# Hedgehog attention and a maxout feed-forward: two heads' last query tokens in one padded tile, part of the first q over a plain queue, and a new order table

## Chip, cores and metric

The kernel runs on one core of one Trainium2 chip. The metric is the device time of one execution in microseconds (us), and lower is better. TensorE is called PE here, VectorE DVE, ScalarE ACT, GpSimd POOL; SyncE (SP) issues transfers only. In a row of the profile, `out<-in` names the tile that is written and the tile that is read, and `L748` is line 748 of the kernel.

## What is computed

Linear attention with a learned feature map, and after it a feed-forward whose hidden layer is the maximum of three products. q, k and v are [8 batches, 8 heads, 576 tokens, 64] in fp32, the hidden width is 768, and the output is [4608, 512].

```python
def phi(x):
    proj = np.einsum('bhsd,df->bhsf', x, w_phi)
    proj = proj - np.max(np.abs(proj), axis=-1, keepdims=True)
    return np.concatenate([np.exp(proj), np.exp(-proj)], axis=-1)
q_p, k_p = (phi(q), phi(k))
kv = np.einsum('bhsf,bhsd->bhfd', k_p, v)
z = np.sum(k_p, axis=2)
num = np.einsum('bhsf,bhfd->bhsd', q_p, kv)
den = np.einsum('bhsf,bhf->bhs', q_p, z)[..., None] + 1e-06
attn = num / den                      # then the heads of a token side by side: x [4608, 512]
h = np.maximum(np.maximum(x @ w1, x @ w2), x @ w3)
return h @ w_out
```

## The kernel before

**Units and chunks.** The attention is done in 16 units: a unit is one batch and four of its eight heads, so units 2b and 2b+1 make batch b. Of a head's 576 tokens 512 are its main tokens, that is four tiles of 128, and the last 64 are its tail. The feed-forward runs in nine chunks of 512 tokens: chunks 0 to 7 take the main tokens of one batch each, chunk 8 the tails of all eight batches.

**Loads.** q and k of a unit are cast to bf16 by the transfer that loads them (`qk_bf`, L383 and L393, issued by POOL). Only unit 0's k comes in as fp32 over SP (`k_raw`, L408) and is cast by DVE and ACT (L415). The tails of q come as fp32 over SP (`tail_raw`, L426, two issues for each pair of units), and POOL casts them into `qk_bf` (L430). v comes as fp32 (`v_raw`, L435).

**Attention of a unit.** Head dimension onto partitions: for units 0 to 3 PE transposes `qk_bf` (`tps`, L459) and DVE or ACT copies the result (`qkT`, L470 and L472); later units use a transposing transfer that SP issues (L478). Then `psk`, `psq`, `pst` = tokens times w_phi (L496), with only 64 of PE's rows in use; the largest magnitude of each token by DVE (`mk`, `mq`, L500); exp of the k features by ACT (`Ek`, L504); v scaled by the tokens' factors `em` on POOL (`vab`, L548); `kvps` = k features times scaled v (L567, 64 rows), copied to `kv_sb` (L574). For q the projection is made the other way round, so that its features lie on partitions (`psm`, L593 with 64 rows, and L600 for the tails), and ACT takes exp of it (`Eq`, L584). The numerators and the denominator are `psn` = Eq times kv_sb (L632), 65 columns for each tile of 128 tokens. They are worked in groups of five tiles, one group for a head: its four main tiles, and the tile that holds its tail and that of its neighbour, of which half goes unused. That makes four groups and 40 matmuls for a unit. DVE joins the two signs (`y`, L641 and L644), inverts the denominator (`rden`, L689), and POOL divides (`x_sb`, L690).

**From x to the output.** x is turned again (`xT`): for units 0 and 1 by PE (`pxT`, L707, copied at L718), and for the others by a transposing transfer of ten blocks (L722, SP). A chunk of the feed-forward takes `ups` = xT times a weight (L748, four matmuls for each of 12 tiles; the first weight enters as differences `w2-w1` and `w3-w1`, made on POOL at L844, and a product of w1 and w_out made once, L855 to L869). DVE or ACT evacuates (L758, L762, L764), then `ops` = the straight product (L781) and the product with w_out (L786), its copy `osb` (L796) and its store (L800, on SP or ACT). The tails of a batch are copied into chunk 8's operand by POOL (L896, L897).

**What sets the order.** Every piece of work is a node, and the table `PLAN` lists all nodes in one sequence, with the engine, the buffers and a time for each; `plan` (L205) reads it. Each engine works through its own nodes in that sequence, and SP's sequence is its queue. So nothing overtakes anything on one engine: an instruction that waits holds up whatever stands behind it there. `fill` (L222) puts matmuls on dummy data (`idler`, L911) between PE's first nodes, where the table's times leave room.

Of the kernel before, what the change touches and what calls it, by code (L numbers as in the profile page):

```python
# [19 lines left out]
P = 128  # L20
# [12 lines left out]
XW = SM + P  # L33
# [4 lines left out]
BY_HALF = 0  # L38
BY_BATCH = 99
# [10 lines left out]
TRAW = 2  # L50
WD_PE = 0
# [37 lines left out]
9G0@1.2 10S0@0.8 3A@1.1 1D@0.8 2G@1.9 16S0@1.3 0G@2.1 103G1@2.7 104G@7.2 4A@1.8 12D@4.0 8G@7.5 6D@4.2 11A@4.0  # L89
19T0@4.5 5A@4.3 7A@4.6 20D0@5.2 25T1@5.8 187S1@2.9 13S@4.5 26D@6.4 29T23@6.3 102G@8.2 30A0@6.7 51T45@6.9 73T67@7.1 110T0@8.0  # L90
105S1@5.1 34A0@7.2 106T1@8.1 18S2@5.7 53D0@7.3 33A@7.7 32D0@7.9 35D@8.5 107D1@9.1 119T53@9.9 75A0@8.2 31A@8.7 260G2@8.9 77A@9.1
74A0@9.6 186G3@9.6 259G@10.4 111D@9.7 76A@10.1 112T21@10.1 188G@11.1 124A1@10.6 123A1@11.1 126T06@10.3 52D@9.9 128A@11.5 17G@11.3 122D1@10.5
115D@11.1 127A@11.8 1166G@11.5 15D@11.7 27T4@12.1 14D@12.0 117A@12.1 120A@12.5 121A@13.0 1167G@12.3 1169G@13.0 130D1@12.2 28D@12.5 43T76@12.8
21T4@13.0 261G@13.8 129D@12.7 46D@13.1 47D@13.5 54A0@13.6 113A@13.8 78T0@13.3 22D@13.8 36T56@14.3 118D@14.1 125D@14.7 56G0@14.0 44A@14.3
114A@14.5 79A@15.0 23T4@14.6 39D@15.3 40A@15.3 24D@15.9 42D@16.3 48T23@16.4 55G@15.1 137A1@15.8 139G1@16.2 80A@16.0 45A@16.2 50D@16.9
116A@16.5 185G@17.3 58A@17.0 108T4@16.7 37A@17.2 334S0@11.6 140G@18.0 263T0@17.2 57A@17.7 59G@18.2 60G@19.3 267T7@17.7 68T13@17.9 61G@20.4
38A@17.8 49D@17.5 81A0@18.3 109D@18.1 264D2@18.7 268D@19.3 41A@18.5 72A@18.9 71A@19.4 138G@20.5 141A@19.9 131T25@18.8 142G@21.6 144A@20.1
62T46@19.1 64A0@20.2 69A@20.3 63A@20.8 70A@21.0 134T07@19.7 132D@19.5 190T3@20.1 65T26@20.6 1168G@22.7 133D@20.1 156T54@21.2 135D@20.7 82T01@21.6
67A@21.4 66A@21.6 161T6@21.9 136D@21.3 158A1@21.7 191D3@21.8 85T27@22.1 159A1@22.2 143G@23.4 83D0@22.4 160A@22.7 86D@22.9 333G0@24.5 157A@23.2
# [156 lines left out]
def kernel(  # L256
# [686 lines left out]
```

## Time and profile before

| | |
|---|---|
| median of three runs | 281.54 us (281.24, 284.22, 281.54) |
| the profiled execution | 282.56 us |
| its span | 280.8 us, so 1.76 us lie around it |
| PE busy | 268.3 us |
| DVE, ACT, POOL busy | 217.3, 199.1, 161.5 us |
| granted clock of PE | 1.0 throughout |

The page gives the busy time of each engine and the span in 40 slices. Groups of instructions have their count, busy time and mean duration. The chain of waits goes back from the last instruction, at each step to what released it. A row of the timeline has start, duration, engine, line and operation. Rows by windows give each engine's busy time in a stretch. An engine that is busy in this sense may still hold a dummy matmul, or a matmul whose end is modelled.

### The profile page before, as it was taken

Reading aid. Unit: us, or ns where it says so; the run is one execution under the profiler, and the core shown is the slowest. Engines: PE = TensorE matmul, PEld = TensorE weight load, DVE = VectorE, ACT = ScalarE, POOL = GpSimd, SP = SyncE. Lnnn points to the kernel's source line nnn. Section 1 sums busy time; section 2 is a strip of 40 time slices with the busy share of each in tenths; the row PEclk is TensorE's granted clock in tenths of the full one; section 3 lists DMA queues with packets and bytes.
Section 4 is the critical chain, followed back from the end, with each engine's and each line's share of the span. In section 5 each row is a group of like instructions: output and inputs, shape, how many; then the busy total and the mean of one; then the engine's idle time right before and its main releaser. Section 6 shows DMA issues by size and latency. Waiting matters only on the chain. (4 is left out here: it accounts for less than half of the span.)

```text
span 280.8 us, 8401 instructions
## 1 busy us (share of the span) xinstructions
PE 268.3 (96%) x3409; PEld 150.8 (54%) x3447; DVE 217.3 (77%) x442; ACT 199.1 (71%) x489; POOL 161.5 (58%) x161
## 2 busy tenths in 40 slices
PE   8789899999999999999999999999999999999993
PEld 5457654576655555555555456655546544444441
DVE  2799989999999969889997899898876871157320
ACT  4799999999999787698978879989589200310001
POOL 4879999998949703897336848393495341000000
PEclk9999999999999999999999999999999999999999
DMA  7999999997999999999999997717130224110253
GB/s 136 300 202 208 207 173 310 260 164 132 171 186 249 236 196 281 169 171 144 189 263 204 188 276 125 151 55 170 39 86 3 77 47 121 40 75 0 82 144 112
DMA packets 76214, 44.52 MB, mean 159 GB/s; under 512 B 52688, under 2 KB 67344, under 8 KB 76176
## 3 DMA queue, kind: packets, MB, share of 16 engines
q1 hardware_dynamic: 59536, 29.21, 49.8%
q0 software_dynamic: 14912, 11.77, 28.7%
q10 hardware_dynamic: 1728, 3.02, 3.0%
q8 instruction: 27, 0.44, 0.7%
q14 instruction: 11, 0.09, 0.1%
HBM read 34.64 MB, written 9.44 MB: 157 GB/s over the span
## 5 line engine op out<-in xcount | busy, mean ns | idle before, releaser
L748 PE MATMUL ups<-xT,w_bf 128*128 128x512 bf16 x414 | 101.3, 379 | 1.0
L584 ACT ACTIVATE Eq<-psm 128x512 bf16<-128x512 f32 (+1 forms) x160 | 81.7, 587 | 5.4 <-PE psm L593 3.1
L548 POOL TENSOR_TENSOR vab<-v_raw,em 128x1152 bf16<-128x1152 f32 (+1 forms) x36 | 68.2, 1907 | 22.9 <-ACT em L542 15.0
L504 ACT ACTIVATE Ek<-psk 128x512 bf16<-128x512 f32 x128 | 72.1, 633 | 8.2 <-PE psk L496 6.3
L748 PEld LDWEIGHTS <-w_bf 128*128 128x128 bf16 x432 | 39.2, 98 | 43.9 <-issue 2.3
L690 POOL TENSOR_TENSOR x_sb<-y,rden 128x640 bf16<-128x640 f32 x32 | 39.9, 1256 | 39.5 <-DVE rden L689 39.0
L786 PE MATMUL ops<-wout_bf,hT 128*128 128x512 bf16 (+2 forms) x214 | 50.5, 373 | 0.3
L758 DVE TENSOR_TENSOR hT<-hT,ups 128x512 bf16<-128x512 bf16 x54 | 35.5, 677 | 13.3 <-PE ups L748 11.1
L500 DVE TENSOR_REDUCE mq<-psq 128x4 f32<-128x512 f32 x64 | 41.2, 682 | 3.5 <-PE psq L496 3.2
L500 DVE TENSOR_REDUCE mk<-psk 128x4 f32<-128x512 f32 x64 | 41.9, 679 | 2.1 <-PE psk L496 1.7
L762 ACT ACTIVATE hT<-ups 128x512 bf16<-128x512 f32 x36 | 21.9, 620 | 24.5 <-PE ups L748 24.4
L641 DVE TENSOR_TENSOR y<-psn,sq 128x325 f32<-128x325 f32 x64 | 30.4, 491 | 6.7 <-PE psn L632 4.3
L796 ACT COPY osb<-ops 128x512 f32<-128x512 f32 x20 | 12.2, 608 | 32.3 <-PE ops L786 31.8
L786 PEld LDWEIGHTS <-hT 128*128 128x128 bf16 x222 | 20.6, 98 | 22.5 <-issue 0.2
L632 PEld LDWEIGHTS <-Eq 128*128 128x128 bf16 x640 | 26.3, 98 | 10.3 <-issue 0.4
L644 DVE TENSOR_TENSOR y<-y,psn 128x325 f32<-128x325 f32 x64 | 29.7, 487 | 1.6
L632 PE MATMUL psn<-kv_sb,Eq 128*128 128x65 bf16 x640 | 28.8, 194 | 0.2
L496 PEld LDWEIGHTS <-qkT 64*128 64x128 bf16 x576 | 18.0, 94 | 13.4 <-issue 8.3
L781 PE MATMUL ops<-xT 128*128 128x512 bf16 x87 | 23.7, 380 | 0.5
L567 PE MATMUL kvps<-vab,Ek 64*128 64x65 bf16 x1152 | 22.1, 191 | 0.8 <-POOL vab L548 0.6
L567 PEld LDWEIGHTS <-Ek 64*128 64x128 bf16 x1152 | 20.3, 94 | 3.4 <-issue 1.3
L796 DVE COPY osb<-ops 128x512 f32<-128x512 f32 (+2 forms) x17 | 11.1, 657 | 12.5 <-PE ops L786 12.5
(65 smaller groups left out, 263.9 us busy)
## 6 DMA issues: line engine op xcount, KB each, us to landing
v_raw<-in_v_dram SPq DMA_DIRECT2D x15, 576.0 KB, 6.0
out_dram<-osb SPq DMA_DIRECT2D x23, 256.0 KB, 3.3
qk_bf<-in_k_dram POOLq DMA_DIRECT2D x15, 288.0 KB, 6.9
qk_bf<-in_q_dram POOLq DMA_DIRECT2D x15, 256.0 KB, 8.7
w_bf<-in_moe_w_dram POOLq DMA_DIRECT2D x3, 768.0 KB, 13.2
out_dram<-osb ACTq DMA_DIRECT2D x9, 256.0 KB, 3.4
tail_raw<-in_q_dram SPq DMA_DIRECT2D x16, 64.0 KB, 4.8
wout_bf<-in_moe_w_out_dram POOLq DMA_DIRECT2D x1, 768.0 KB, 19.2
```

What stands on the lines that cost most here:

```text
L500: return nd(kind, {"DVE": 0.598 if n == 4 else 0.331}, lambda: nc.vector.tensor_reduce(dst(m()), ps()[:, 0:n, :], AXX, ALU.max, apply_abso ...
L504: return nd("ek", {"ACT": 0.478 if n == 4 else 0.264}, lambda: nc.scalar.activation(dst(Ek[g]()), ps()[:, 0:n, :], EXP, scale=1.0 - 2.0 * ...
L548: made.append(chosen(n_, lambda n_, g=g, t0=t0, t1=t1: (nc.vector if n_.eng == "DVE" else nc.gpsimd).tensor_tensor(vab()[:, g, t0:t1, 0:D] ...
L567: nc.tensor.matmul(kvps[ab]()[:, pr, g, :], lhsT=Ek[g]()[r, t, :], rhs=vab()[r, g, t, :], start=(pr == prs[0] and g + j == 0), stop=(pr == ...
L584: return nd("eq", {"ACT": 0.478 if n == 4 else 0.264}, lambda: nc.scalar.activation(Eq[g]()[:, t0:t0 + n, :], ps()[:, 0:n, :], EXP, scale= ...
L632: nc.tensor.matmul(psn[g]()[:, i, :], lhsT=Eq[g]()[:, t, :], rhs=kv()[:, pr, ab, g, :], start=True, stop=True)
L641: n_ = nd("xu", {"DVE": 0.064 + 0.0676 * n_t}, lambda: nc.vector.tensor_tensor(yv(y()), ps(0), sq_of(sq()).unsqueeze(len(shape) - 1).to_br ...
L644: return nd("xw", {"DVE": 0.064 + 0.0674 * n_t}, lambda: nc.vector.tensor_tensor(yv(y()), yv(y()), ps(1), ALU.add), [n_], [psn[1], y], loc ...
L690: divs[pr] = nd("x", {"POOL": 1.2}, lambda pr=pr, y=y, rden=rden: nc.gpsimd.tensor_tensor(x_sb()[:, pr].rearrange("p t a d -> p a t d"), y ...
L748: nc.tensor.matmul(ups()[:, o * n:(o + 1) * n], lhsT=w_bf[i + (not plain)][:, ct, jj * P:(jj + 1) * P], rhs=tokens_of(ct)[:, cols] if halv ...
L758: nc.vector.tensor_tensor(dst, dst, src, ALU.max)
L786: nc.tensor.matmul(ops_()[:, 0:hi - lo], lhsT=hT()[:, j, tt * P:(tt + 1) * P], rhs=wout_bf[:, j, lo:hi], start=plain and j == 0, stop=(j = ...
```

## The change

- **Tails.** The tail tiles of two heads are combined before the numerators. `eq_ends` holds exp of the tails' q features with 64 zeroed columns between two heads' tails, so that an operand of 128 columns has one head's tail and zeros beside it. Two matmuls add up into one tile, which then has the tails of two heads. A unit so has 18 tiles instead of 20, still with 40 matmuls.
- **Groups.** Numerators go in three groups of six tiles (390 columns) instead of four of five (325), and two of them are main tiles only. DVE's join, the inverse and POOL's division have three pieces for a unit; the division had two. `sq` takes one activation instead of two. xT has nine blocks for a unit instead of ten, and PE turns units 0 and 1 in three groups of three blocks. The copy at the tails' end into chunk 8's operand takes one instruction instead of two.
- **Loads and stores.** q of the first two heads of unit 0 comes as fp32 over SP (`q_raw`) and DVE casts it in two pieces. Tails are loaded for each unit, two issues of 32 KB, where it was two of 64 KB for two units; there are four buffers for them instead of two. For units 0 to 3 the tails' cast may go to DVE or ACT, and the scaling of v to DVE. All of v and all full stores are issued by SP; before, one v and nine of these stores were on ACT.
- **Order.** `PLAN` is new throughout. Options that had been switched off are gone from the code.

The diff, cut to its core; of the table it shows one line each.

```diff
-XW = SM + P
+XB = PT * P
...
+PLAIN_Q = 1
...
-TRAW = 2
+TRAW = 4
...
-9G0@1.2 10S0@0.8 3A@1.1 1D@0.8 2G@1.9 16S0@1.3 0G@2.1 103G1@2.7 104G@7.2 4A@1.8 12D@4.0 8G@7.5 6D@4.2 11A@4.0
+13S0@0.8 1D@0.8 4A@1.1 0G@1.2 16S@1.3 3G@1.7 5A@1.8 19S0@1.9 12G0@2.2 2G@2.9 107G1@3.1 266S1@3.5 14D@4.0 7A@4.1
...
-    xT = const.tile([P, B, CT, XW], BF16, name="xT")
+    xT = const.tile([P, B, 2, XB], BF16, name="xT")
+    eq_ends = const.tile([P, ES, 2, 2, 3, ST], BF16, name="eq_ends")
...
+    n_zero = node("zero", 0, {"DVE": 0.25, "POOL": 0.45}, None, [], [], port=True)
+    chosen(n_zero, lambda n_: (nc.vector if n_.eng == "DVE" else nc.gpsimd).memset(
+        eq_ends.rearrange("p e g r z c -> p (e g r) z c")[:, :, 1, :], 0.0))
...
+        for p0, p1 in ((0, 1), (1, 2)) if u == 0 else ((0, 2),):
+            if u > 0 or p0 >= PLAIN_Q:
+                main_q.append([nd("Lq", {"POOL": 0.72}, lambda p0=p0, p1=p1: load_q(p0, p1), [], [qk_b],
+                                  xfer=[(16 * (p1 - p0), 44.0, 0.72)])])
+                continue
+            n_ = nd("Lq", {"SP": 0.42, "ACT": 0.58}, None, [], [qraw], xfer=[(16, 44.0, 0.42)])
+            chosen(n_, lambda n_, p0=p0: queue_of[n_.eng].dma_start(
+                qraw()[:, 8 * p0:8 * p0 + 8, :].rearrange("p (h j) d -> p h (j d)", j=SM // P),
+                q[b, h0 + 2 * p0:h0 + 2 * p0 + 2, 0:SM, :].rearrange("h (p j) d -> p h (j d)", p=P)))
+            parts = []
+            for t0 in (8 * p0, 8 * p0 + 4):
+                c_ = nd("Cq", {"DVE": 0.206, "ACT": 0.3}, None, [n_], [qraw, qk_b], port=True)
+                parts.append(chosen(c_, lambda c_, t0=t0: copy_on[c_.eng](qs()[:, t0:t0 + 4, :], qraw()[:, t0:t0 + 4, :])))
+            main_q.append(parts)
...
-        if u % 2 == 0:
-            t_raw = tails["raw"] = buf("tail_raw", TRAW, [P, 2 * HU // 2, D], FP32)
-
-            def load_t(n_):
-                ends = q[b, :, SM:S, :].rearrange("(pr ab) i d -> ab i pr d", ab=2)
-                for ab in range(2):
-                    queue_of[n_.eng].dma_start(t_raw()[ab * D:(ab + 1) * D, :, :], ends[ab])
-            tails["load"] = chosen(nd("Lt", {"SP": 1.24}, None, [], [t_raw], xfer=[(16, 18.0, 0.62)] * 2), load_t)
-        t_raw = tails["raw"]
-        n_ = nd("C", {"POOL": 0.233}, None, [tails["load"]], [t_raw, qk_b], port=True)
+        t_raw = buf("tail_raw", TRAW, [P, 2, D], FP32)
+
...
+        def load_t(n_):
+
+            ends = q[b, h0:h0 + HU, SM:S, :].rearrange("(a r) i d -> a i r d", r=2)
+            for a in range(2):
+                queue_of[n_.eng].dma_start(t_raw()[a * ST:(a + 1) * ST], ends[a])
+        n_t = chosen(nd("Lt", {"SP": 1.24}, None, [], [t_raw], xfer=[(8, 18.0, 0.62)] * 2), load_t)
+        n_ = nd("C", {"POOL": 0.24, "DVE": 0.13, "ACT": 0.17} if by_pe else {"POOL": 0.24}, None, [n_t], [t_raw, qk_b], port=True)
         tail = chosen(n_, lambda n_: copy_on[n_.eng](
             ks().rearrange("p (r j) d -> p r j d", j=PT + 1)[:, :, PT, :],
-            t_raw()[:, 2 * (u % 2):2 * (u % 2) + 2, :]))
+            t_raw()))
         vraw = buf("v_raw", RAW, [P, UT, D], FP32, of="raw")
-        main_v = chosen(nd("Lv", {"SP": 0.42, "ACT": 0.6}, None, [], [vraw], xfer=[(16, 93.0, 0.42)]),
+        main_v = chosen(nd("Lv", {"SP": 0.42}, None, [], [vraw], xfer=[(16, 93.0, 0.42)]),
                         lambda n_: queue_of[n_.eng].dma_start(
...
+                if u < BY_PE:
+                    costs["DVE"] = 0.064 + 0.0667 * (t1 - t0)
                 n_ = nd("va", costs, None, [n_em, main_v], [vraw, em, vab], port=True)
                 made.append(chosen(n_, lambda n_, g=g, t0=t0, t1=t1: (nc.vector if n_.eng == "DVE" else nc.gpsimd).tensor_tensor(
...
-        eqs["t"] = [q_exp(a, psm, 2, g, NQ) for g in range(2)]
-        x_sb = buf("x_sb", XSB, [P, 2, 5, 2, D], BF16)
...
+        eqs["t"] = [nd("eq", {"ACT": 0.264}, lambda g=g: nc.scalar.activation(
+            Et()[:, g, :, 0:3:2, :], psm()[:, 0:2, :].rearrange("p r (z c) -> p r z c", z=2), EXP, scale=1.0 - 2.0 * g),
+                       [a, n_tab], [psm, Et], locks=[psm]) for g in range(2)]
+
+
+        sq = buf("sq", MS, [P, UT], FP32)
+        n_sq = nd("S", {"ACT": 0.1}, lambda: nc.scalar.activation(sq(), mq(), EXP, scale=-2.0), reds_q, [mq, sq])
+        x_sb = buf("x_sb", XSB, [P, UT, D], BF16)
+        divs = []
+        for th in range(3):
+            mine = range(6 * th, 6 * th + 6)
+            ends = th == 2
+            prs = range(2) if ends else sorted({t // 8 for t in mine})
+            psn = [bank("psn", [P, 6, W]) for _ in range(2)]
+
+            def nmm(mine=mine, psn=psn):
+                for i, t in enumerate(mine):
+                    for g in range(2):
+                        o = psn[g]()[:, i, :]
+                        if t < NQ:
+                            pr, c, ab = t // 8, t // 2 % 4, t % 2
+                            nc.tensor.matmul(o, lhsT=Eq[g]()[:, 8 * (c % 2) + 4 * pr + 2 * ab + c // 2, :], rhs=kv()[:, pr, ab, g, :],
                                              start=True, stop=True)
-                        i += 1
...
+                            continue
+                        for pr in range(2):
+                            pad = Et()[:, g, t - NQ, pr:pr + 2, :].rearrange("p z c -> p (z c)")
+                            nc.tensor.matmul(o, lhsT=pad, rhs=kv()[:, pr, t - NQ, g, :], start=(pr == 0), stop=(pr == 1))
+            need = [n for pr in prs for n in n_kvs[pr]] + [n for pr in ((1,) if ends else prs) for n in eqs[pr]]
+            a = nd("N", {"PE": 0.0313 * (16 if ends else 12)}, nmm, need + (eqs["t"] + [n_zero] if ends else []),
+                   Eq + [kv] + [Et] * ends + psn)
+            y = buf("y", YS, [P, 6, W], FP32)
+            rden = buf("rden", YS, [P, 6, 1], FP32)
+            n_ = nd("xu", {"DVE": 0.064 + 0.0676 * 6}, lambda th=th, y=y, psn=psn: nc.vector.tensor_tensor(
+                y(), psn[0](), sq()[:, 6 * th:6 * th + 6].unsqueeze(2).to_broadcast([P, 6, W]), ALU.mult), [a, n_sq], [psn[0], sq, y],
                     locks=[psn[0]])
...
+            n_ = nd("xw", {"DVE": 0.064 + 0.0674 * 6}, lambda y=y, psn=psn: nc.vector.tensor_tensor(y(), y(), psn[1](), ALU.add),
+                    [n_], [psn[1], y], locks=[psn[1]])
+            n_ = nd("xr", {"DVE": 0.108}, lambda y=y, rden=rden: nc.vector.reciprocal(rden(), y()[:, :, D:W]), [n_], [y, rden])
+            n_ = nd("x", {"POOL": 0.767, "DVE": 0.464} if by_pe else {"POOL": 0.767}, None, [n_], [y, rden, x_sb], port=True)
+            divs.append(chosen(n_, lambda n_, th=th, y=y, rden=rden: (nc.vector if n_.eng == "DVE" else nc.gpsimd).tensor_tensor(
+                x_sb()[:, 6 * th:6 * th + 6, :], y()[:, :, 0:D], rden().to_broadcast([P, 6, D]), ALU.mult)))
 
...
+            for th in range(3):
+                pxT = bank("pxT", [P, 3, P], BF16)
+                def tx(th=th, pxT=pxT):
+                    for o in range(3):
+                        t = 6 * th + 2 * o
+                        nc.tensor.transpose(pxT()[:, o, :], x_sb()[:, t:t + 2, :].rearrange("p a d -> p (a d)"), ident)
...
+                nc.sync.dma_start_transpose(out=xT[:, b, u % 2, :].rearrange("p (t c) -> p t c", c=P),
+                                            in_=x_sb().rearrange("p t d -> p (t d)"))
+            done.append(nd("X", {"SP": 1.21}, xdma, divs, [x_sb], xfer=[(72, 18.0, 1.21)]))
...
-                    s_ = ff("store", {"SP": 0.41, "ACT": 0.6} if n_out == 1 else {"SP": 1.2}, None, [e], [osb],
+                    s_ = ff("store", {"SP": 0.41} if n_out == 1 else {"SP": 1.2}, None, [e], [osb],
...
     def last(b):
-        nc.gpsimd.tensor_copy(xT[D:P, b, :, SM:SM + ST], xT[D:P, b, :, SM + ST:XW])
-        nc.gpsimd.tensor_copy(x_last[b // 4][:, :, b % 4 * ST:(b % 4 + 1) * ST], xT[:, b, :, SM:SM + ST])
+        nc.gpsimd.tensor_copy(x_last[b // 4][:, :, b % 4 * ST:(b % 4 + 1) * ST].rearrange("p (u c) n -> p u c n", u=2),
+                              xT[:, b, :, 2 * SM:XB].rearrange("p u (c n) -> p u c n", n=ST))
     for b in range(B):
-        lasts.append(node("C", 2 * b + 1, {"POOL": 0.8}, lambda b=b: last(b),
+        lasts.append(node("C", 2 * b + 1, {"POOL": 0.42}, lambda b=b: last(b),
```

At the start of DVE's sequence the table changes what stands between unit 0 and unit 1. Names: `qk_bf<-k_raw` is unit 0's k, the copies `qkT<-tps` are transposed blocks, the reductions `mk`, `mq` the largest magnitudes. Before, from the first cast on:

```order
L415 CAST qk_bf<-k_raw 128x320
L337 CAST wph<-wphi_f 64x128
L472 COPY qkT<-tps 128x512 x2
L500 TENSOR_REDUCE mq<-psq 128x4
L500 TENSOR_REDUCE mk<-psk 128x4 x2
L470 COPY qkT<-tps 128x2x512
L470 COPY qkT<-tps 128x2x128
L500 TENSOR_REDUCE mq<-psq 128x4
```

After, the same place:

```order
L407 CAST qk_bf<-k_raw 128x256
L341 CAST wph<-wphi_f 64x128
L461 COPY qkT<-tps 128x512
L341 CAST wph_low<-wphi_f 64x128
L491 TENSOR_REDUCE mk<-psk 128x4 x2
L459 COPY qkT<-tps 128x2x128
L461 COPY qkT<-tps 128x512
L491 TENSOR_REDUCE mk<-pst 128x2
L461 COPY qkT<-tps 128x512
L491 TENSOR_REDUCE mq<-pst 128x2
L491 TENSOR_REDUCE mk<-psk 128x4
L459 COPY qkT<-tps 128x2x512
```

The first copy of `128x2x512`, which is unit 1's k, had five instructions ahead of it after the first two casts; now it has ten, unit 0's tail and the second half of its k among them.

The second place is SP's sequence around the transposing transfers of x of units 2 and 3 (`xT<-x_sb`). Before:

```order
L478 DMA_TRANSPOSE qkT<-qk_bf 128x10x128
L435 DMA v_raw<-in_v_dram 128x2x576 x2
L478 DMA_TRANSPOSE qkT<-qk_bf 128x8x128
L722 DMA_TRANSPOSE xT<-x_sb 128x10x128
L478 DMA_TRANSPOSE qkT<-qk_bf 128x10x128
L478 DMA_TRANSPOSE qkT<-qk_bf 128x8x128
L722 DMA_TRANSPOSE xT<-x_sb 128x10x128
L478 DMA_TRANSPOSE qkT<-qk_bf 128x10x128
```

After:

```order
L467 DMA_TRANSPOSE qkT<-qk_bf 128x10x128
L426 DMA v_raw<-in_v_dram 128x2x576
L418 DMA tail_raw<-in_q_dram 64x2x64 x2
L426 DMA v_raw<-in_v_dram 128x2x576
L467 DMA_TRANSPOSE qkT<-qk_bf 128x8x128 x3
L654 DMA_TRANSPOSE xT<-x_sb 128x9x128
L467 DMA_TRANSPOSE qkT<-qk_bf 128x10x128
L654 DMA_TRANSPOSE xT<-x_sb 128x9x128
L418 DMA tail_raw<-in_q_dram 64x2x64 x2
L467 DMA_TRANSPOSE qkT<-qk_bf 128x10x128
```

One transfer stands between the two of x where two did, but three stand directly ahead of the first where it was one.

More of the change, by code (lines that the diff above doesn't have):

```diff
@@ L341 @@
     units = [dict() for _ in range(UNITS)]
-    tails, loads, qk_bufs = {}, {}, [None]
     def k_rows(src, u, p0, p1):
@@ L442, in attention @@
             need_k = [main_k[0], main_k[1]]
[L443 to L444 removed]
+            if u == 0:
+                need_q = main_q
                 parts = [(("k0",), k_of[0], main_k[0]), (("k1",), k_of[1], main_k[1]),
```

480 lines of the change are left out of this document (169 added, 311 removed).

## The prediction

> **What bounds the kernel.** I read the page first: busy times, the slices, the shares of the chain of waits.
>
> ```profile
> span 280.8 us, 8401 instructions
> PE 268.3 (96%) x3409; PEld 150.8 (54%) x3447; DVE 217.3 (77%) x442; ACT 199.1 (71%) x489; POOL 161.5 (58%) x161
> ...
> PE   8789899999999999999999999999999999999993
> ...
> PE 44%; POOL 1%; issue 0%; ACT 0%; ACTq 0%
> ```
>
> PE is busy for 96% of the span and in nearly every slice after the first five. The chain consists of PE almost alone. Its rows in order of time show where it starts and ends, and the price of one detail:
>
> ```profile
> 150.90 1.95 POOL vab L548
> ...
> 152.89 1.04 PE kvps L567 x54
> ...
> 156.87 0.11 PE psm L600
> ...
> 170.65 0.22 PE psm L593 x2
> ...
> 178.16 0.33 PE psq L496 x8
> 178.49 0.22 PE psk L496 x8
> ...
> 273.63 2.60 PE ops L786 x12
> ...
> 276.30 0.59 ACT osb L796
> ```
>
> From 152.9 us to 276.2 us PE never waits for anything but itself, so there only fewer or cheaper matmuls help. The two rows at 178 us have the same eight matmuls. The first row follows matmuls that use all 128 rows of PE and costs 0.11 us more: that is a switch between 64 and 128 rows.
>
> Next come the stretches (columns: length, busy time and count of PE, PEld, DVE, ACT, POOL, then clock, DMA share, GB/s), with the first feed-forward matmuls from the timeline:
>
> ```profile
> 3.88:39.84 35.96, 32.02 (x525) 21.86 (x526) 31.36 (x70) 32.18 (x85) 31.03 (x35) 1.00 1.19 216
> 40.81:276.24 235.43, 232.55 (x2869) 126.67 (x2903) 184.79 (x369) 164.08 (x401) 127.03 (x117) 1.00 0.78 151
> ...
> 40.81 1.03 PE L748 MATMUL ups<-xT,w_bf 128*128 128x512 bf16 x4
> ```
>
> From 40.81 us, the first `ups`, to PE's end PE idles for 235.43 - 232.55 = 2.9 us in all. Before that the kernel works up to the first `ups`: DVE is busy for 31.36 of 35.96 us (4.6 us idle) up to the last copy of x of unit 1, which chunk 0 needs, and PE pads with dummy matmuls. So the time is made of four parts: the start up to the first `ups` (DVE's pace), 232.6 us of PE work, 2.9 us of PE waiting, and 280.8 - 276.24 = 4.6 us of tail.
>
> **Part 1: the start.** Counted in the order of instructions, DVE has 81 instead of 72 instructions up to the last copy of `xT<-pxT`. Prices:
>
> ```profile
> L500 DVE TENSOR_REDUCE mk<-psk 128x4 f32<-128x512 f32 x64 | 41.9, 679 | 2.1 <-PE psk L496 1.7 <-ACT Ek L504 0.3
> L641 DVE TENSOR_TENSOR y<-psn,sq 128x325 f32<-128x325 f32 x64 | 30.4, 491 | 6.7 <-PE psn L632 4.3 <-PE psm L600 1.5 <-ACT Eq L584 0.8
> L644 DVE TENSOR_TENSOR y<-y,psn 128x325 f32<-128x325 f32 x64 | 29.7, 487 | 1.6
> L500 DVE TENSOR_REDUCE mk<-pst 128x2 f32<-128x256 f32 x16 | 6.6, 410 | 0.4 <-PE pst L496 0.3
> L689 DVE RECIPROCAL rden<-y 128x10 f32<-128x10 f32 x32 | 6.4, 206 | 0.2
> L718 DVE COPY xT<-pxT 128x640 bf16<-128x640 bf16 x3 | 1.4, 481 | 0.0
> L470 DVE COPY qkT<-tps 128x256 bf16<-128x256 bf16 x4 | 1.1, 286 | 0.2
> L415 DVE CAST qk_bf<-k_raw 128x256 bf16<-128x256 f32 x1 | 0.3, 286 | 0.0
> ```
>
> - Four more reductions of 512 columns, 4 x 0.68, and one of 256, 0.41: +3.1 us. These are pieces of units 2 and 3 that the new table puts earlier.
> - The two reductions differ by 269 ns over 256 columns, 1.05 ns a column, so 65 more columns cost 0.07 us. The join takes 12 x (0.49 + 0.07) = 6.7 us instead of 16 x 0.49 = 7.8: -1.1 us.
> - Two more inverses: +0.4 us.
> - Six more small casts (three pieces of `kv_sb`, two tails, one of w_phi), each below the 0.29 of a cast of 256 columns; at 0.25: +1.5 us. The two casts of q (2 x 0.29) stand against two k casts that go to ACT, and one 1024-column copy more against one less: 0.
> - Three xT copies of 384 instead of 640 columns; by the two copy rows about 0.5 ns a column, taken as 0.2 us each with the fixed part: -0.5 us.
>
> Together about +3.3 us of DVE work. What of it can go into the idle time is read from the waits:
>
> ```profile
> PE tps L459 <- DMA qk_bf<-in_k_dram: 1.6, 1, 1.6
> DVE qkT L470 <- PE tps L459: 1.3, 1, 1.3
> ...
> DVE mk L500 <- PE psk L496: 0.4, 1, 0.4
> ```
>
> PE waits 1.6 us for unit 1's k, and DVE then 1.3 us for its transposes. In the new order the tail and second half of unit 0 stand ahead of this copy, ten instructions instead of five, so this wait is covered; so is the 0.4 us of the projection behind it. 3.3 - 1.7 = **+1.6 us**. The ends: all 4.6 us of idle time filled, -1.3; none, +3.3. I take the middle, since the order shows cover for these two waits only.
>
> **Part 2: PE's work after the first `ups`.** By the order, 16 more `psq` (two rows of eight as at 178.49, 0.44 us), two more `psm` of 512 columns and one of 256 now stand ahead of the first `ups`. By the rows of the chain these cost 0.22 for two and 0.11, so 0.77 us with the `psq`. That work is gone from behind: **-0.8 us**. The start has room for it, since it drops seven dummy matmuls. The count of `psn` matmuls stays at 640 by 65 columns. Switches between 64 and 128 rows after the first `ups` fall from 74 to 68, counted in the order: 6 x 0.11 = **-0.65 us**.
>
> **Part 3: waits of PE.** Of the 2.9 us one is named:
>
> ```profile
> PE kvps L567 <- POOL vab L548: 0.6, 1, 0.6
> ```
>
> I leave them as they are: **0**, with -0.6 (this wait goes) and +3.5 (below) as ends.
>
> **Part 4: everything beside PE.** These cost nothing while PE is the bound from 41 us on (232.6 of 235.4 us), which is their cover; each would cost its full size if PE had to wait for it.
>
> ```profile
> L690 POOL TENSOR_TENSOR x_sb<-y,rden 128x640 bf16<-128x640 f32 x32 | 39.9, 1256 | 39.5 <-DVE rden L689 39.0 <-PE psn L632 0.4
> L548 POOL TENSOR_TENSOR vab<-v_raw,em 128x1152 bf16<-128x1152 f32 x28 | 59.1, 2123 | 20.4 <-ACT em L542 12.5 <-issue 6.4 <-DMA v_raw<-in_v_dram 1.6
> L548 POOL TENSOR_TENSOR vab<-v_raw,em 128x576 bf16<-128x576 f32 x8 | 9.1, 1154 | 2.5 <-ACT em L542 2.5
> L610 ACT ACTIVATE sq<-mq 128x4 f32<-128x4 f32 x16 | 3.6, 227 | 0.0
> L896 POOL COPY xT<-xT 64x256 bf16<-64x256 bf16 x8 | 3.2, 398 | 4.0 <-DMA xT<-x_sb 3.5
> ```
>
> - DVE: join 48 x 2 x 0.556 = 53.4 us instead of 30.4 + 29.7, about -7, inverses +3: -4 us.
> - POOL: the scaling of v gives 1.68 ns a column and 0.19 us fixed, so a division of 384 columns takes 0.83 us, and 48 of them 39.9 us, what 32 take now: 0. L896 goes: -3.2 us. Zeroing `eq_ends`: one memset at the start.
> - ACT: the second activation of `sq` goes, -3.6 us, and nine stores.
> - Stores: the last one moves from ACT's to SP's queue; both are a short issue and a landing: 0.
>
> **Part 5: SP's queue.**
>
> ```profile
> 63.80 1.34 SPq L722 DMA_TRANSPOSE xT<-x_sb  x1
> 65.24 2.99 SPq L478 DMA_TRANSPOSE qkT<-qk_bf  x2
> 69.10 1.35 SPq L722 DMA_TRANSPOSE xT<-x_sb  x1
> ...
> 75.41 0.82 PE L748 MATMUL ups<-xT,w_bf 128*128 128x512 bf16 x2
> ...
> DMA to landing us min/median/max: 3.3/3.6/7.2
> ...
> L426 SPq DMA_DIRECT2D tail_raw<-in_q_dram x16: 602/618/747, 1.2 to 152.9; - x16
> ```
>
> Sixteen more tail issues at 0.62 us are 9.9 us of SP, ten of them ahead of x of unit 3. Also ahead of it: unit 0's q, and one v less. x of unit 3 is issued at 69.10 and with the median landing there at 72.7; chunk 1's first `ups` starts at 75.41. So 2.7 us are to spare. SP has gaps before 63.8 us in which it waits for casts and loads, and there the ten issues fit; the transfers directly between the two of x fall from two to one. I take 0, with 6.2 - 2.7 = +3.5 as the upper end.
>
> **The sum:** +1.6 - 0.8 - 0.65 + 0 + 0 = +0.15, say +0.2 us. The profiled execution took 282.56 us (span 280.8), so its counterpart is 282.8. It lies 1.0 above the median of the runs, and the difference applied to that median, 281.54, gives **281.7 us**.
>
> **Rivals.**
>
> *Slower: x of unit 3 comes late on SP.* Place: the queue around 63 to 72 us. Three transposing transfers now stand directly ahead of unit 2's x, each some 1.5 us of SP (2.99 for two), and the ten tail issues come out of the same queue. It decides once x of unit 3 is over 2.7 us later against PE; then chunk 1's `ups` hold all of PE's work behind them, and PE's order can't go round it. With all 6.2 us of the issues late: 281.7 + 3.5 = 285.2 us. For it: the two rows of x stand in a burst with no gap in SP. Against it: SP issues only four transposing transfers in 8 us there, and one of them leaves from between the two of x.
>
> *Faster: the start doesn't get longer.* All of DVE's 4.6 us fill up (-1.3), because the new loads of tails and of half of q let nothing wait at the start; the wait for `vab` at 151 us goes as well. -1.3 - 0.8 - 0.65 - 0.6 = -3.3, 278.2 us. For it: 1.6 us of PE's wait is for a transfer of the very kind that the plain load relieves on POOL's queue. Against it: the waits of DVE that are left are for PE's results, which the new order doesn't bring earlier by itself.
>
> *DVE's new SBUF work shuts POOL out.*
>
> ```profile
> L548 POOL TENSOR_TENSOR vab<-v_raw,em x36: 1143/2122/2162, 15.8 to 210.6; 128x1152 bf16<-128x1152 f32 x28, 128x576 bf16<-128x576 f32 x8
> L844 POOL TENSOR_TENSOR w_bf<-w_bf x6: 2110/2122/2132, 29.3 to 45.2; 128x1024 bf16<-128x1024 bf16 x6
> ```
>
> One scaling of v of 1152 columns and four casts move to DVE with all their operands in SBUF: by the join's row and 1.05 ns a column 0.49 + 827 x 1.05/1000 = 1.36 us, and 4 x 0.25, together 2.4 us. If POOL stands still for all of it and x of unit 1 comes later by as much: 281.7 + 2.4 = 284.1 us. Against it: POOL's durations hardly spread (2110 to 2132 ns) at a time at which DVE is busy too, though that DVE work mostly reads PSUM. The Trainium skill states this as a rule, page "SBUF — State Buffer", section "SBUF: two separate sides": a VectorE operation in a two-port mode or with two SBUF inputs holds the port pair that it shares with GpSimd for the whole instruction, and GpSimd is blocked. By that rule this rival is what happens; no row of this trace has such a VectorE operation beside POOL.
>
> *The change saves what it names, on engines that don't bound,* and nothing shows: that is the forecast, near enough.
>
> **Chances.** A measurement of this kernel can tell about 1% from no change: below 278.7 is faster, above 284.35 slower. The forecast with its neighbours within 1%: 0.62, and the blocked POOL 0.08, which ends inside 1% too: same 0.70. x of unit 3 late, 0.18, is slower. The shorter start, 0.12, is faster. The range: 278.8 to 285.2. It takes in the ends of part 1 (278.8 with -1.3, 283.4 with +3.3) and the late x up to its price, and leaves out the full faster case and an x that comes later still.
>
> **What would show it.** First `ups` at 42.4 us (40.81 + 1.6), and PE's end 233.9 us behind it (235.4 - 0.8 - 0.65). Longer than 235.4 means a new wait, and the waits of PE name it: `ups` for x of unit 3 in the first rival. POOL rows of 1152 columns well above 2.16 us early on would show the third. A first `ups` before 40.8 us would prove part 1 wrong; a last PE end more than 4.6 us before the span's end the tail.

## The result: 3.8% slower, and the profile after

The changed kernel takes 292.56 us (median of five runs, 291.74 to 296.54), against 281.54 for the kernel before beside it (five runs, 281.24 to 284.22). The ratio is 1.0376, with an interval from 1.0331 to 1.0421. The forecast was 281.7 us and its range ended at 285.2, so the time lies outside it. The profiled execution took 294.42 us with a span of 292.6. (Ratios here leave out disturbed executions; medians and their spans take in all of them.)

The page of the changed kernel, as far as it answers to the lines shown of the kernel before:

```profile
span 292.6 us, 8396 instructions
PE 271.9 (93%) x3398; PEld 153.7 (53%) x3438; DVE 220.5 (75%) x434; ACT 198.2 (68%) x475; POOL 154.3 (53%) x163
...
PE   8966999999659999999999999999999999999993
...
PEclk9996999999959999999999999999999999999999
...
PE 80%; ACT 5%; POOL 4%; issue 4%; DVE 3%; DMA 3%; POOLq 0%; DVEq 0%; ACTq 0%
```

PE had 9 in nearly every slice; now it dips twice, in the third and fourth slices (15 to 29 us) and in the eleventh and twelfth (73 to 88 us), and in the second slice of each pair the granted clock dips as well. The other engines moved by less: DVE's busy time grew by 3.2 us, less than the 4.0 that a single cast, shown below, took too long; ACT's fell by 0.9 and POOL's by 7.2. The prediction's prices for the new shapes held too, as the groups show (busy, mean ns of one):

```profile
L629 DVE TENSOR_TENSOR y<-psn,sq 128x390 f32<-128x390 f32 x48 | 26.2, 557 | 5.2 <-PE psn L618 4.1
L632 DVE TENSOR_TENSOR y<-y,psn 128x390 f32<-128x390 f32 x48 | 26.3, 556 | 2.4
L636 POOL TENSOR_TENSOR x_sb<-y,rden 128x384 bf16<-128x384 f32 x48 | 39.0, 824 | 52.8 <-DVE rden L634 50.8
```

The waits of PE name both places (total, times, longest):

```profile
PE tps L448 <- DVE qk_bf L421: 4.8, 2, 4.4
PE psk L487 <- DMA qkT<-qk_bf: 4.5, 1, 4.5
PE ups L675 <- DMA xT<-x_sb: 1.3, 1, 1.3
```

And the windows give the account (length, then busy time and count of PE, PEld, DVE, ACT, POOL, then clock). The first two rows are the stretches up to the first `ups` and from there to PE's end; the other four are each dip, its idle part first:

```profile
0.00:47.35 47.35, 39.35 (x551) 27.21 (x554) 39.22 (x81) 36.98 (x92) 34.95 (x45) 0.93 1.12 198
47.35:288.14 240.79, 232.57 (x2849) 126.48 (x2885) 181.27 (x353) 160.65 (x383) 119.39 (x119) 0.99 0.76 142
19.85:23.56 3.71, 0.00 (x1) 0.00 (x0) 3.71 (x2) 1.01 (x3) 3.71 (x5) 1.00 1.15 204
23.56:30.39 6.83, 6.10 (x80) 4.42 (x82) 5.82 (x11) 4.55 (x12) 3.45 (x5) 0.50 1.22 208
77.90:81.59 3.69, 0.01 (x2) 0.00 (x0) 1.28 (x3) 0.86 (x2) 3.59 (x5) 1.00 1.44 159
81.59:88.42 6.83, 4.72 (x28) 2.27 (x30) 2.01 (x4) 3.73 (x9) 0.00 (x0) 0.50 1.32 190
```

The span grew by 292.6 - 280.8 = 11.8 us. The first `ups` went from 40.81 to 47.35 (+6.5), the stretch behind it from 235.43 to 240.79 (+5.4), and the tail from 4.56 to 4.46. Each dip begins with 3.7 us in which PE does nothing. Then the clock is at half for 6.83 us, in the first 0.7 and 0.8 us of which PE still waits.

**The first dip.** The timeline of the changed kernel, DVE first, then POOL, then PE:

```profile
19.71 0.28 DVE L568 CAST kv_sb<-kvps 128x130 bf16<-128x130 f32 x1
19.91 4.27 DVE L421 CAST qk_bf<-tail_raw 128x128 bf16<-128x128 f32 x1
24.01 0.68 DVE L461 COPY qkT<-tps 128x1024 bf16<-128x1024 bf16 x1
...
19.25 0.77 POOL L374 DMA_DIRECT2D qk_bf<-in_q_dram  x1
20.02 3.40 POOL L542 TENSOR_TENSOR vab<-v_raw,em 128x576 bf16<-128x576 f32 x3
23.35 0.81 POOL L738 DMA_DIRECT2D w_bf<-in_moe_w_dram  x1
24.14 0.75 POOL L374 DMA_DIRECT2D qk_bf<-in_q_dram  x1
...
24.24 0.39 PE L448 MATMUL tps<-ident,qk_bf 128*128 128x128 bf16 x2 [4.38 <-DVE qk_bf L421]
```

One small cast on DVE, that of unit 2's tails, takes 4.27 us where a cast of nearly the same width out of PSUM takes 0.28. It begins at 19.91, inside POOL's issue of a q load (to 20.02), and ends at 24.18, with POOL's issue of the w_bf load (to 24.16); in between POOL runs three scalings of v without a pause. PE waits for the cast's tile. POOL's own three scalings take 1.13 us each, as before (1154 ns).

**The second dip.** SP's queue, then POOL, then PE, in the timeline of the changed kernel:

```profile
65.71 7.06 SPq L467 DMA_TRANSPOSE qkT<-qk_bf  x3
72.87 1.36 SPq L654 DMA_TRANSPOSE xT<-x_sb  x1
74.32 1.80 SPq L467 DMA_TRANSPOSE qkT<-qk_bf  x1
76.21 3.77 SPq L654 DMA_TRANSPOSE xT<-x_sb  x1
...
74.05 0.77 POOL L379 DMA_DIRECT2D qk_bf<-in_k_dram  x1
...
82.42 0.61 PE L487 MATMUL psk<-wph,qkT 64*128 64x128 bf16 x8 [4.51 <-DMA qkT<-qk_bf]
...
84.85 1.01 PE L675 MATMUL ups<-xT,w_bf 128*128 128x512 bf16 x2 [1.28 <-DMA xT<-x_sb]
```

The transposing transfers of k of unit 6 (74.32) and of x of unit 3 (76.21) leave SP late, and land late. From issue to landing they took, in this order:

```profile
DMA to landing us min/median/max: 8.1/8.1/8.1
...
DMA to landing us min/median/max: 8.6/8.6/8.6
```

In the kernel before the same transfer of x, issued at 69.10, took 5.1 us:

```profile
DMA to landing us min/median/max: 5.1/5.1/5.1
```

PE first misses k of unit 6, which the prediction hadn't looked at, and then x of unit 3, its slower rival.

### The profile page after: what moved, and what is told of

Read it like the earlier page. It is cut to its first block, busy times and chain, and to the rows that moved or that the text cites. A ratio compares the mean times of both kernels' runs of the same rounds, so it can differ in the third digit from the quotient of the medians.

```text
span 292.6 us, 8396 instructions
## 1 busy us (share of the span) xinstructions
PE 271.9 (93%) x3398; PEld 153.7 (53%) x3438; DVE 220.5 (75%) x434; ACT 198.2 (68%) x475; POOL 154.3 (53%) x163
## 4 chain that ended last, share of the span: by engine, by line
PE 80%; ACT 5%; POOL 4%; issue 4%; DVE 3%; DMA 3%; POOLq 0%; DVEq 0%; ACTq 0%
PE ups L675 30%; PE ops L712 15%; PE ops L707 10%; PE kvps L561 5%; PE psn L618 5%; DMA xT<-x_sb 3%; PE idler L817 3%; PE psk L487 3%; PE psm L587 2%; ACT Ek L495 2%; PE psq L487 2%; POOL vab L542 2%; PE pm L775 2%; PE psn L623 1%; DVE mq L491 1%
## 5 line engine op out<-in xcount | busy, mean ns | idle before, releaser
L495 ACT ACTIVATE Ek<-psk 128x512 bf16<-128x512 f32 x128 | 74.3, 642 | 15.7 <-PE psk L487 10.9
L578 ACT ACTIVATE Eq<-psm 128x512 bf16<-128x512 f32 x128 | 70.8, 626 | 8.5 <-PE psm L587 8.3
L636 POOL TENSOR_TENSOR x_sb<-y,rden 128x384 bf16<-128x384 f32 x48 | 39.0, 824 | 52.8 <-DVE rden L634 50.8
L688 ACT ACTIVATE hT<-ups 128x512 bf16<-128x512 f32 x32 | 19.1, 624 | 27.7 <-PE ups L675 27.7
L720 ACT COPY osb<-ops 128x512 f32<-128x512 f32 (+2 forms) x25 | 14.5, 588 | 27.6 <-PE ops L712 21.1
L629 DVE TENSOR_TENSOR y<-psn,sq 128x390 f32<-128x390 f32 x48 | 26.2, 557 | 5.2 <-PE psn L618 4.1
L690 DVE TENSOR_SCALAR hT<-ups 128x512 bf16<-128x512 f32 x22 | 14.8, 685 | 18.8 <-PE ups L675 18.7
L632 DVE TENSOR_TENSOR y<-y,psn 128x390 f32<-128x390 f32 x48 | 26.3, 556 | 2.4
L618 PEld LDWEIGHTS <-Eq 128*128 128x128 bf16 x512 | 22.1, 100 | 8.7 <-issue 1.0
L618 PE MATMUL psn<-kv_sb,Eq 128*128 128x65 bf16 x512 | 24.4, 196 | 0.1
```

The lines of the kernel that those rows point to most:

```text
L495: return nd("ek", {"ACT": 0.478 if n == 4 else 0.264}, lambda: nc.scalar.activation(dst(Ek[g]()), ps()[:, 0:n, :], EXP, scale=1.0 - 2.0 * ...
L578: return nd("eq", {"ACT": 0.478 if n == 4 else 0.264}, lambda: nc.scalar.activation(Eq[g]()[:, t0:t0 + n, :], ps()[:, 0:n, :], EXP, scale= ...
L618: nc.tensor.matmul(o, lhsT=Eq[g]()[:, 8 * (c % 2) + 4 * pr + 2 * ab + c // 2, :], rhs=kv()[:, pr, ab, g, :], start=True, stop=True)
L636: divs.append(chosen(n_, lambda n_, th=th, y=y, rden=rden: (nc.vector if n_.eng == "DVE" else nc.gpsimd).tensor_tensor(x_sb()[:, 6 * th:6 ...
```

## The experiments

Three theories were to be told apart. The first: DVE's cast is shut out by POOL, and SP's new order makes two operands late; each costs its wait. The second: the waits are cheap and the half clock behind them is the cost. The third, as in the prediction's slower rival: the tail issues fill SP. Table rows are given as the words of `PLAN` that differ: node, engine with its buffer, time (T is PE, D DVE, A ACT, G POOL, S SP). Line numbers differ between the kernels. The runs come from several sessions, and each ratio is to the kernel before in the same session; differences of medians against the 292.56 us of the changed kernel go across sessions.

**Unit 2's tail cast on ACT.**

```diff
-194D@18.9
+194A@18.9
```

> The changed kernel with one letter of the table altered: the cast of unit 2's tail goes to ACT instead of DVE, at the same place. Theory 'lock': the cast took 4.27 us on DVE only because POOL worked beside it on SBUF without a pause; on ACT it takes about 0.4 us, PE's wait of 4.4 us for it and the half clock after it go, the first feed-forward matmul comes near 42 us instead of 47.35, and the time falls by 4 to 6 us to 286.5 to 288.5, with the later wait at unit 6's k and unit 3's x still there. Rival 'data late': the cast waited for its tail or its buffer; then ACT's cast is late as well, the first feed-forward matmul stays near 47 us and the time near 292. Rival 'one cause': all of the later loss follows from the late start; then the time falls to 280 to 283.

Measured: 286.66 us, ratio 1.0133 (1.009 to 1.0176): 5.9 less than the changed kernel. The cast on ACT stands beside the same POOL run (three scalings in 3.40 us):

```profile
19.82 0.29 ACT L441 CAST qk_bf<-tail_raw 128x128 bf16<-128x128 f32 x1
...
20.16 0.28 PE L468 MATMUL tps<-ident,qk_bf 128*128 128x128 bf16 x2 [0.49 <-ACT qk_bf L441]
```

The first `ups` is at 41.65 and the first dip of the clock is gone; the second dip stays, with a wait of 4.6 us for k of unit 6. So 5.9 of the 11.0 us of loss hang on the engine of one cast; by the ratios it is 2.4 of 3.8%. This run's profiled execution took 289.65, 3.0 above the median, and its half clock at the second dip lasted 10.24 us, so that dip is probably larger in it than in the usual run.

**Two q transposes behind unit 3's x.** The three transposing transfers at 65.71 us are q of units 7, 6 and 5, and PE needs the first two only from 94 us on.

```diff
-550S2@57.3
...
-481S3@58.7
...
-480S@62.8
+480S3@62.8
...
+481S@64.5
+550S2@64.9
```

> The changed kernel with two transposing transfers of q (units 7 and 6, first needed by PE at 94 us or later) moved in SP's queue from ahead of unit 2's x to behind unit 3's x. Theory 'queue': PE's waits of 4.5 us for unit 6's k and 1.3 us for unit 3's x came from these two standing ahead; both go and with them the half clock from 81.6 to 88.4 us (about 3 us of work lost): 283 to 286. Rival 'transfers slow': the transfers land late because the data side was slow around 75 to 79 us whatever the order; then PE waits there as long as before and the time is 290 to 293.

Measured: 289.04 us, ratio 1.0229 (1.0181 to 1.0277), 1.5% less than the changed kernel's. PE goes through the place without a wait:

```profile
77.50 0.39 PE L507 MATMUL psk<-wph,qkT 64*128 64x128 bf16 x8
77.81 1.04 PE L695 MATMUL ups<-xT,w_bf 128*128 128x512 bf16 x4
```

The place is right. The gain in medians, 3.5 us, is less than expected; in the profiled executions it was 292.6 - 287.1 = 5.5. The changed kernel's own profiled execution was 1.9 above its median, so the second dip may be larger in it than in the usual run.

**Both.** The two edits together.

> Both edits together, unit 2's tail cast on ACT and the two q transposes behind unit 3's x. If the two causes are independent, the gains add up: 278 to 282, clock 1.0 from the first feed-forward matmul to the last. Rival 'one cause': the second edit adds nothing to the first, or something else that was hidden behind both waits is late next; then within 2 us of the better of the two single edits.

Measured: 283.09 us, ratio 1.0014 (0.9977 to 1.0051). 5.9 and 3.5 add up to 9.4, and together they brought 9.5. By the ratios it is 2.4 and 1.5% against 3.6% together, so the two losses are independent within the intervals, and the closer agreement of the medians is chance. The windows of the kernel before up to its first `ups`, then of this kernel up to its first and from there to PE's end:

```profile
0.00:40.81 40.81, 35.76 (x542) 24.14 (x545) 32.49 (x74) 34.43 (x88) 34.42 (x45) 1.00 1.13 205
...
0.00:41.21 41.21, 36.70 (x553) 25.40 (x554) 34.82 (x80) 36.70 (x93) 34.78 (x45) 1.00 1.17 209
41.21:277.15 235.94, 233.36 (x2887) 125.99 (x2885) 180.67 (x353) 160.80 (x383) 119.37 (x119) 1.00 0.78 148
```

**Dummy matmuls while PE waits.** Everything as in the changed kernel, with 36 matmuls on dummy data ahead of the two waiting nodes; first each with a tile of its own in the same bank.

```diff
+    for i in (200, 482):
+        fed(nodes[i], 36)
```

> The changed kernel with 36 dummy matmuls of 256 columns (3.9 us of PE) ahead of the transposes of unit 2's tail and 36 ahead of the projection of unit 6's k, where PE sat idle for 4.4 and 4.5 us. The waits stay, only PE isn't idle in them. Theory 'clock': the two stretches of 6.8 us at half clock follow from PE's idleness; they vanish, the granted clock is 1.0, and the time falls by what PE lost in them, 3 to 5 us: 287.5 to 289.5. Rival: half clock has another cause (it stays) or cost nothing since PE wasn't the bound there: 291 to 293.

Measured: 310.35 us, ratio 1.0993 (1.0966 to 1.1019): a miss. The dummies came far apart, and the clock fell all the same:

```profile
19.32 13.28 PE L837 MATMUL idler<-idle 128*128 128x256 bf16 x36
```

36 in 13.28 us is one every 0.37 us, and from 25.79 us to 36.02 the granted clock was 0.50. Matmuls of 256 columns that far apart didn't hold it. So the dummies were put into one tile, where they follow each other without a wait:

> The dummy matmuls of the earlier run again, this time all 36 of a place into one PSUM tile so that they follow each other at about 0.11 us each, not 0.37. The two waits of PE stay; PE isn't idle in them. Theory 'clock': both stretches of half clock vanish, granted clock 1.0, time 3 to 5 us below 292.56: 287.5 to 289.5. Rival: half clock stays, or cost nothing because PE wasn't the bound in it: 291 to 293.

Measured: 289.45 us, ratio 1.027 (1.0232 to 1.0308). The page's row of the clock, and the first dummies:

```profile
PEclk9999999999999999999999999999999999999999
...
19.14 4.09 PE L825 MATMUL idler<-idle 128*128 128x256 bf16 x36
```

The clock stays up, the cast still takes 4258 ns, and the time falls by 292.56 - 289.45 = 3.1 us. That is the price of the half clock at both places (1.1% by the ratios); the other 8 us are the waits themselves. The second theory explains the smaller part.

**The same cast on DVE as a reduction.** What in the cast is shut out: any work of DVE in SBUF, or this form? The cast stays on DVE at its place and is written as a maximum over an axis of one element.

```diff
+            if u == 2:
+                nc.vector.tensor_reduce(dst, t_raw().unsqueeze(3), AXX, ALU.max)
```

> The changed kernel with unit 2's tail cast still on DVE, at the same place, but written as a maximum over an axis of one element instead of a copy; the values are the same. Theory 'lock by the copy's mode': a plain copy from SBUF to SBUF needs the port that POOL uses, a reduction doesn't; the reduction takes 0.2 to 0.5 us, PE's wait of 4.4 us goes, first feed-forward matmul near 42 us, time 285 to 288 as with the cast on ACT. Rival 'any DVE work between SBUF tiles is shut out': it takes about 4 us again, time 291 to 294. Rival 'data late': the same 4 us.

Measured: 288.04 us in the median of nine runs, which scatter from 283.24 to 289.39; ratio 1.0049 (1.0009 to 1.0088). The time says little, and the trace decides. The timeline of this kernel, DVE's reduction and POOL's run beside it:

```profile
19.33 0.27 DVE L424 TENSOR_REDUCE qk_bf<-tail_raw 128x128 bf16<-128x128 f32 x1
...
19.43 3.40 POOL L546 TENSOR_TENSOR vab<-v_raw,em 128x576 bf16<-128x576 f32 x3
```

The same operands, the same engine and a start 0.1 us before the same POOL run: 0.27 us instead of 4.27. The first `ups` comes at 41.11, and what is left of the loss in this execution (285.74) are waits of 2.1 and 1.9 us for k of unit 6 and x of unit 3. So not every work of DVE between SBUF tiles is shut out: the cast's form is, and this reduction isn't.

**The cast alone, in the kernel before.** Only unit 2's tail cast moves from POOL to DVE there, and in the table to the time at which POOL scales v without a pause.

```diff
-188G@11.1
+188D@20.3
```

> The kernel before, with one part of the change alone: unit 2's tail cast on DVE instead of POOL, placed in DVE's order where POOL scales v of units 0 and 1 without a pause (20 to 26 us). Theory 'lock': the cast of 128 columns takes 2 to 5 us instead of 0.3, DVE's work behind it and the first feed-forward matmul come later by as much, 283 to 287 against 281.5 to 282.7. Rival 'the new table only': here the cast takes 0.3 us and the time is that of the kernel before.

Measured: 285.66 us, ratio 1.0137 (1.0091 to 1.0183). DVE's cast, and POOL beside it:

```profile
22.07 2.86 DVE L430 CAST qk_bf<-tail_raw 128x128 bf16<-128x128 f32 x1
...
21.90 2.25 POOL L548 TENSOR_TENSOR vab<-v_raw,em 128x576 bf16<-128x576 f32 x2
24.10 0.81 POOL L814 DMA_DIRECT2D w_bf<-in_moe_w_dram  x1
```

The cast again ends (24.93) when an issue of a w_bf load ends (24.91), and not between the two scalings. PE waits 2.3 us for DVE's reductions, which come late behind the cast, and for the cast's own tile not at all; so the later place in the table doesn't show as a cost. One word of the table costs this kernel 1.4% by itself, with nothing else of the change in it.

**Why the transfers land late.** POOL issues a casting load (one that casts to bf16 on the way) of k of unit 8 at 74.05, just ahead of the two late transposes. First that load 3 us later, on the changed kernel:

```diff
-614G0@65.8
+614G0@71.0
```

> The changed kernel with one casting load on POOL's queue (unit 8's k, issued at 74.05 us) moved behind two scalings of v, about 5 us later. In the changed kernel the transposes of unit 6's k issued at 74.32 took 8.1 us to land and those of unit 3's x at 76.21 took 8.6, against medians of 6 and 3.4. Theory 'load beside transposes': this load's packets hold up the transposes; without it both land in 3.5 to 5 us, PE's wait of 4.5 us shrinks to 0 to 1.5, and the time falls by 4 to 7 us (its half clock goes too): 285.5 to 288.5. Theory 'queue order alone': landing stays near 8 us and the time is 290.5 to 293.

Then, with the load left where it is, two tail issues taken out of the queue ahead of these transposes:

```diff
-822S2@55.1
+822S2@65.5
```

> The changed kernel with the two tail issues that stand directly ahead of the burst (unit 11's, 63.6 to 64.9 us on SP's queue) moved behind unit 3's x. Theory of the prediction's slower rival, that the added tail issues at 0.62 us each are what makes unit 3's x late: 1.3 us less ahead of it, PE's wait of 4.5 us falls to about 3.2 and the time by 1 to 2 us. Rival: the queue waits for casts and landed data anyway, and the issues only fill its gaps; no change, 291.5 to 293.

Measured: 288.66 us, ratio 1.0217 (1.0177 to 1.0257), for the load; 290.28 us, ratio 1.0276 (1.0239 to 1.0312), for the issues. With the load at 77.19, SP's queue and the two landings (k of unit 6, then x of unit 3):

```profile
72.76 1.40 SPq L467 DMA_TRANSPOSE qkT<-qk_bf  x1
74.25 1.42 SPq L654 DMA_TRANSPOSE xT<-x_sb  x1
...
DMA to landing us min/median/max: 3.5/3.5/3.5
...
DMA to landing us min/median/max: 4.9/4.9/4.9
```

They land in 3.5 and 4.9 us instead of 8.1 and 8.6, and only a wait of 1.9 us for x is left. (This execution is 1.4 us ahead of the changed kernel's at the first `ups` already, at 45.91; landings are counted from each issue, so they don't depend on it.) With the two issues moved, k of unit 6 is issued at 73.20, 1.0 us ahead of the load at 74.20, and lands in 3.6; x is issued at 74.78, behind the load, and lands in 6.9, with a wait of 2.7. So the tail issues cost about what the prediction said of them, 2 x 0.62 = 1.2 us (here 74.32 to 73.20 and 76.21 to 74.78), but the larger part is what comes of it: behind the casting load a transpose lands 2 to 5 us later than 1 us or more ahead of it.

Two rows of other runs belong beside this. An issue just ahead of the load doesn't help: k of unit 6 left 0.05 us ahead of it in the run with the reduction and 0.08 us ahead in the run with the dummies in one tile, and landed in 6.7 and 8.5 us. And the load needn't be a casting one: with the two q transposes moved, q of unit 5 and x of unit 2 left at 64.66 and 66.08 behind a plain load of v (63.97), with no casting load since 57.10, and landed in 6.8 and 6.5 us.

**Further from there.** On the kernel with both repairs, unit 11's load of v goes behind unit 5's x; and on that one the k load of unit 8 is moved too.

```diff
-824S3@91.8
+824S3@95.2
```

> Both repairs together, and the load of unit 11's v (first used 60 us later) moved on SP's queue from ahead of unit 5's x to behind it and one transpose. With both repairs alone, chunk 2's first matmul waits 1.1 us for unit 5's x, whose transfer took 8.1 us to land, and 0.6 us for the next transposes. Theory 'queue': with 576 KB less ahead of it x lands about 1.4 us earlier and most of the 1.7 us goes: 0.5 to 1.5 us below the run with both repairs, so 0 to 1 us faster than the kernel before. Rival: the wait moves to the next late transfer, no gain.

> The repaired kernel with unit 11's v behind unit 5's x (the fastest so far, 281.52 against 282.25 before), and with unit 8's k load 5 us later as in the run above. If the load holds up transposes, later waits shrink by another 0 to 1 us: 280.5 to 281.5. If it doesn't matter, or makes unit 8 late, 281.3 to 283.

Measured: 281.52 us, ratio 0.9967 (0.9945 to 0.9989) for the first, the fastest of all; 282.85 us, ratio 1.0025 (0.9998 to 1.0052) with the load moved too, so no further gain. In the profiled execution of the latter (281.36, 1.5 below its median) PE has no wait above 0.5 us behind the first `ups`, and the windows show PE's bare pace there:

```profile
41.83:275.06 233.23, 232.96 (x2887) 125.89 (x2885) 180.67 (x353) 160.61 (x383) 119.25 (x119) 1.00 0.77 150
```

## Why the prediction was wrong

- **Part 1, the start: failed.** It said +1.6 us, between -1.3 and +3.3; measured was +6.5. The step that failed is "Six more small casts [...] at 0.25", the price of an instruction alone. One of them cost 4.27 us, for what POOL did at that time. Without that wait the step was sound: first `ups` at 41.65, 41.11 and 41.21 with the cast on ACT, as a reduction, and with both repairs, that is +0.3 to +0.8. DVE's extra work up to there, 34.82 - 32.49 = 2.3 us with both repairs, moved the first `ups` by 0.4 only; the rest went into idle time, more than the half that I took.
- **The third rival: right port, wrong side.** It let POOL stand still for DVE's 2.4 us. At this place POOL wasn't delayed at all; DVE waited for the whole run of POOL's instructions. The Trainium skill, page "SBUF — State Buffer", section "SBUF: two separate sides", says that the pair of ports is an exclusive lock, taken by whichever starts first, for the whole instruction. The traces agree that it is exclusive and that not every form takes it (0.27 us for the reduction). The prediction gave only the half of this rule in which DVE holds the pair. Here POOL was first, for the cast began inside POOL's issue of a load, and it waited for more than one instruction: three scalings and a further issue passed before it was done. POOL's side of it shows once, at 54.49 us: a scaling of 2.74 us instead of 2.12 beside DVE's scaling of unit 2's v. That is 0.6 us, with no wait of PE behind it; the DVE scaling took 1.79 us, where the prediction's estimate was 1.36.
- **Part 2, PE's work: right.** 235.43 - 0.8 - 0.65 = 233.9 us was forecast without any change in waits, and 233.23 was measured where all waits behind the first `ups` were gone. The 2.9 us of idle PE in the kernel before weren't all waiting, as the prediction had it: beside the last run, its trace lacks the records of 36 matmuls behind the first `ups` (18 of 432 `ups`, 18 of `ops`). With `ups` 0.216 us apart and 0.379 us long, a missing one shows as 2 x 0.216 - 0.379 = 0.05 us of idle time, 1.9 us in all by this estimate, and 1.9 us is what the trace has as idle time ahead of `ups` and `ops`. That leaves 1.0 us of waits before and 0.27 in the last run, so of 235.43 - 233.23 = 2.2 us some 1.5 are work, as 0.8 + 0.65 forecast. The two terms are confirmed together, not one by one.
- **Parts 3 and 5, SP's queue: failed in size.** "So 2.7 us are to spare" was worked with the median landing of 3.6 us. The landing of that very transfer stood in the trace: 5.1 us, so 1.2 us were to spare. The slower rival had the place, the queue at 63 to 72 us, and the operand; it priced the tail issues alone. What made the operands late was the order of two q transposes that nobody needed for 20 us (moved: 3.5 us less) and the load beside them (8.1 and 8.6 us instead of 3.5 and 4.9). I read the new order for what stands ahead of x, and not for what stands ahead of k of unit 6.
- **The clock: missing.** The prediction has no term for it. After 3.7 us of idle PE, in waits of 4.4 and 4.5 us, came 6.83 us at 0.50, twice, which cost 3.1 us in all. The Trainium skill, page "TensorE: Matmul & The Clock Gate", section "🔬 Part 1: The HAM clock gate (the "warmup" mystery)", says that an idle window of about 3.4 us halves PE's clock; these rows agree. Shorter waits did it as well: 1.9 us with the load moved and 2.3 us in the kernel before with the one cast on DVE were each followed by 3.41 us at half clock, and 1.1 us with both repairs by none. So a wait has a step in its price, and the upper end of a range has to have it too. The half clock behind these two waits, first with the load moved, then with the one cast:

```profile
79.20:82.60 3.40, 3.40 (x19) 1.65 (x19) 1.87 (x4) 1.78 (x5) 1.22 (x2) 0.50 1.08 150
...
26.70:30.10 3.40, 3.34 (x56) 2.50 (x55) 2.43 (x7) 1.27 (x5) 0.85 (x2) 0.51 1.25 206
```

- **Part 4 and the tail: right.** 0.557 and 0.556 us for the joins, 0.824 for the division, 4.46 us behind PE's end; nothing beside PE showed. ACT's busy time fell by 0.9 us and not by 3.6; it stayed covered.

With its two faults repaired the change makes next to no difference: +0.1% (both repairs), -0.3% (with the v load moved too) and +0.25% (with the k load moved as well). That is what the sum, +0.2 us, said of the change that I had in mind, and not of the one with this order table.

Open are these. Why a load slows transposing transfers isn't shown, only that moving it does away with most of the delay. How POOL's issue of a load holds off the cast isn't clear: the two long casts end with such an issue, and so does a third, of another unit's tail in the changed kernel, which ran beside issues alone (0.47 us from 14.20, where the issue of a k load ends at 14.65); but a cast of q of 256 columns behind it took 0.27 us inside the next issue. And why the two q transposes brought 5.5 us in the profiled executions but 3.5 in the medians isn't settled.

## What to carry to other kernels

A small operation that moves to another engine is priced by what runs beside it at its new time, not by its own duration: look at what POOL does there before a copy from SBUF to SBUF goes to DVE, and give it to ACT, or write it as another form. The spare time of a transfer is worked out with its own landing, and a new order on a queue is read for every operand behind the place, with the loads that run beside it. An idle share of PE is worth comparing with the count of its records before it is called waiting. A wait of PE of some 2 us or more cost more than its length in these runs, so the end of a range has a step there.

## What the hardware showed that was not expected

- DVE's cast of 128 columns from SBUF to SBUF took 4.27, 4.26 and 2.86 us beside an unbroken run of POOL instructions, and the same data through a reduction 0.27 us. POOL's scalings beside it took 1.13 us each, as without it.
- Stretches at half clock came as 3.41 us (the load moved), 6.83 (the changed kernel), 10.24 and 13.65 (the dummies 0.37 us apart), multiples of one length of 3.41. Dummy matmuls of 256 columns every 0.37 us didn't prevent them, and such matmuls back to back, one every 4.09 / 36 = 0.11 us, did.
- Transposing transfers landed in 6.9 to 8.6 us when issued behind a casting load, in 6.7 and 8.5 when issued less than 0.1 us ahead of it, and in 3.5 to 5.1 when about 1 us or more ahead. Behind a plain load of v two of them took 6.8 and 6.5.
